# The head loads of a fused S5 scan and GEGLU kernel: w_gate in three column parts, one up row in one piece, token tile 3 earlier in the queue, and a new order of all engines

## The chip, the cores and the metric

The kernel runs on one core of a Trainium2 chip. The metric is the device time of one execution in microseconds (us). Three executions of the kernel before took 178.48 to 178.82 us, median 178.79.

## What is computed

`x` has 2048 tokens of 512 channels, all tensors are bfloat16. The reference, cut to what matters:

```python
xn  = (x - mean(x)) / sqrt(var(x) + 1e-5)            # per token
# A: a diagonal state space model over the tokens, 512 complex states
dt = exp(log_dt); Lam_bar = exp(dt * Lam)
B_bar = ((Lam_bar - 1.0) / Lam)[:, None] * Bmat
h = Lam_bar * h + B_bar @ xn[t]                      # for t = 0 .. 2047
s[t] = 2.0 * (Cmat @ h).real + xn[t] * Dskip
# B: a gated feed-forward block of 1376 columns
g = silu((gelu(xn @ w_gate) * (xn @ w_up)) @ w_down)
out = x + s * g
```

## The kernel before

**Tiling.** The tokens form 4 slabs of 512, each of 4 tiles of 128. The 1376 columns of w_gate and w_up are three chunks: 0 to 512 (chunk 0), 512 to 1024 (chunk 1, up to `W2`), and the last 352 (chunk 2). `W1` is 512.

**Slab 0's head.** Nothing is loaded when the kernel starts, so slab 0 is done in small steps. SyncE (SP) issues the loads of token tiles and weights in one queue (`load_x` L296, `load_w` L287, `load_slab` L291). The first token tile is centred by VectorE in two halves (L418), the other three get their sums from ScalarE (L423) and are centred by VectorE (L424). TensorE transposes each centred tile (L387 for tile 0 in two pairs of 128 columns, L400 for the others), VectorE or ScalarE copies the transposed tile to `W` (L391, L393, L402). Then `up_rows` (L462) multiplies one 128-row slice of w_up, one chunk and one tile per matmul, 32 in all, in an order that follows the arrival of the rows. `first_w` (L499) takes the remaining up products (chunk 2) and then all gate products of slab 0, four matmuls per tile and chunk, each group followed on ScalarE by a scaled copy (L471) or the gelu (L505) that empties its PSUM bank. `gated` (L518, VectorE) multiplies the two.

**The steady part.** From then on the tokens come normalised (`norm`, sums by ScalarE L848 for slabs 2 and 3, normalisation L853) and transposed by a DMA (`dma_t4`, L436, tile `xnT`). For each tile there are gate and up products (`gate_tile`, L536, emptied at L539), a DMA transpose of the gated activations (`at_t`, L551), and the product with w_down (`down_pair`, L564, silu at L567). For each slab `half` forms the 512 complex inputs of the scan in 16 products of four matmuls (L621) with the transposed B_re and B_im (loaded at L314); ScalarE empties their banks to `U` (L623), VectorE rotates (L638), scans (L657) and rotates back (L646 and L650) to the states `hst`. `y_part` multiplies the states with `C2` (L579), and VectorE multiplies with the silu and adds x (L586, L587) before the output DMA (L592). The last output tile of all comes in three pieces of 160, 160 and 192 columns. Tables of cosines and sines for the rotation are made early by `tables` (L707 on GpSimd, L708 on ScalarE, L719 on VectorE).

**What sets the order.** All of this is recorded as some 695 numbered steps in a class `Plan`, each with its engine, what it reads and writes, and its buffer group. `Plan.run` emits them in the order of the table `ORDER`; the table `SLOTS` gives each buffer group its buffer: `ps` six PSUM banks, `pp` two more, and the rest SBUF buffers. An engine executes its steps in exactly that order, so a step that waits holds up what stands behind it on the same engine. The queue order of the loads is set by `ORDER` too, not by the place of the `load_` call in the code.

Of the kernel before, what the change touches and what calls it, by code (L numbers as in the profile page):

```python
# [18 lines left out]


ORDER = (
# [24 lines left out]
)  # L46
SLOTS = {
# [4 lines left out]
    ),  # L52
    "pp": (
        0, 0, 1, 0, 1, 1, 0, 1, 0, 0, 1, 0, 0, 1, 1, 1, 1, 1, 0, 0, 0, 0, 0, 0, 1, 1, 1, 0, 1, 0, 0, 0, 1, 1, 0, 1, 1, 1, 1,
    ),
    "U": (
        0, 1, 2, 3, 0, 1, 2, 3,
    ),
    "g2": (
        0, 1, 4, 5, 3, 5, 1, 2, 0, 3, 4, 2, 0, 1, 5, 4,  # L60
    ),
    "at": (
        1, 0, 3, 2, 0, 2, 1, 1, 0, 3, 2, 3, 0, 2, 1, 1,
    ),
    "gtA": (
        0, 1, 1, 0, 1, 1, 0, 0, 1, 1, 0, 1, 0, 1, 0, 1,
    ),
    "gtB": (
        0, 1, 0, 1, 1, 0, 0, 1, 0, 1, 1, 1, 0, 0, 0, 1,
    ),  # L70
    "ubA": (
        1, 1, 0, 0, 1, 0, 1, 1, 1, 0, 1, 0,
    ),
    "ubB": (
        1, 1, 0, 0, 0, 1, 1, 1, 0, 0, 0, 1,
    ),
    "yg": (
        0, 1, 1, 0, 0, 0, 1, 0, 1, 1, 0, 0, 1, 0, 0, 1, 1, 0, 1,
    ),
    "ot": (  # L80
        1, 1, 0, 0, 0, 0, 0, 0, 1, 0, 0, 0, 0, 1, 1, 1, 0,
    ),
    "sk": (
        2, 3, 1, 0, 6, 5, 7, 4, 2, 1, 0, 3, 5, 6, 4, 7,
    ),
    "atT": (
        1, 0, 2, 2, 0, 1, 3, 3, 3, 0, 2, 2, 0, 3, 1, 1,
    ),
}

# [58 lines left out]
def kernel(  # L149
# [21 lines left out]
    F = 1376  # L171
    KT = D // P
# [23 lines left out]
    def sb(name, shape, dt=BF16):  # L196
        return consts.tile(shape, dt, name=name)
# [3 lines left out]
    wg = sb("wg", [P, KT, F])  # L201
    wu = sb("wu", [P, KT, F])
# [10 lines left out]
    W2 = CH[1][1]  # L213
# [51 lines left out]
    def dma(eng, issue, land, emit, reads=(), writes=(), **kw):  # L265
        return pl.add(eng, issue, emit, reads, writes, lag=land, **kw)
# [11 lines left out]
    def dma_sp(end, landed, emit, writes, **kw):  # L278

        n = dma(SP, end - sp_at[0], landed - end, emit, writes=writes, after=list(sp_last), not_before=sp_at[0], svc=(1, 0.0, 0.0), **kw)  # L280
        sp_at[0] = end
        sp_last[:] = [n]

    def load_w(nm, k0, k1, c0, c1, end, landed):

        w, r = w_of[nm]
        dma_sp(end, landed, lambda: nc.sync.dma_start(out=w[:, k0:k1, c0:c1], in_=r[:, k0:k1, c0:c1]),  # L287
               [(nm, k, c) for k in range(k0, k1) for c in range(3) if c0 <= CH[c][0] < c1])
# [6 lines left out]
    def load_x(m, end, landed):  # L295
        dma_sp(end, landed, lambda: nc.sync.dma_start(out=x_tok[:, m, :], in_=x_r[:, m, :]), [("x", 0, m)])  # L296

    W1 = CH[0][1]
# [5 lines left out]
    load_w("wu", 1, 2, 0, W1, 3.47, 5.5)  # L304
    load_w("wu", 1, 2, W1, W2, 3.94, 6.05)
    load_x(3, 4.41, 6.6)
    load_w("wu", 2, 3, 0, W1, 4.88, 7.15)
    load_w("wu", 2, 3, W1, W2, 5.35, 7.7)
    load_w("wu", 3, 4, 0, W2, 5.82, 8.8)
    load_w("wu", 0, KT, W2, F, 6.29, 10.0)  # L310
    load_w("wg", 0, KT, W1, F, 6.76, 12.4)
    load_w("wg", 0, KT, 0, W1, 7.23, 14.0)
    for ri, src in enumerate((A_B_re, A_B_im)):
        dma(SP, 2.0, 3.0, lambda ri=ri, src=src: nc.sync.dma_start_transpose(out=BT[:, ri, :, :], in_=src), writes=[("BT", ri)],  # L314
            after=list(sp_last), svc=TURN)
# [614 lines left out]
```

## Time and profile before

| | |
|---|---|
| median of three runs | 178.79 us (178.48 to 178.82) |
| the profiled execution | 179.01 us |
| its span, first to last instruction | 177.2 us |
| TensorE busy | 172.8 us (97%) |
| VectorE busy | 155.0 us (87%) |
| ScalarE busy | 125.7 us (71%) |
| GpSimd busy | 10.7 us (6%) |

The profile is of one execution and starts its clock at the first instruction; 1.81 us of the execution's own time lie around the span. Its views: the chain of work that ended last, followed back from the last instruction; the timeline, in which each row is a run of like instructions on one engine (start, length, line, number, and in brackets the idle time ahead with what ended it); the busy time of each engine in chosen windows; and the DMA issues with the median time to landing. "SPq" is the issue of a DMA by SyncE, "PEld" a weight load of TensorE, which runs beside its matmuls. Two timeline rows of pipelined instructions can overlap, so the distance of two starts says more than a length.

### The profile page before, as it was taken

The numbers are of one execution on the slowest core, as the hardware profiler recorded it, in microseconds if no ns is written. First come the engines' busy times: TensorE is split into PE (matmuls) and PEld (weight loads), VectorE is DVE, ScalarE is ACT, GpSimd is POOL, SyncE is SP. The second block draws the span as 40 slices with busy tenths as digits, with TensorE's granted clock in tenths as the row PEclk, the third lists the DMA queues.
The fourth block names the chain that finished last, engine by engine and source line by source line (L and its number), as shares of the span: only waits on it lengthen the run. The fifth ranks groups of instructions, "written<-read, shape, count | busy, mean of one in ns | idle before, by whom it ended". The sixth has DMA issues, their size and how long they took to land.

```text
span 177.2 us, 2445 instructions
## 1 busy us (share of the span) xinstructions
PE 172.8 (97%) x857; PEld 82.6 (47%) x857; DVE 155.0 (87%) x255; ACT 125.7 (71%) x242; POOL 10.7 (6%) x25
## 2 busy tenths in 40 slices
PE   7999999999999999999999999999999999999993
PEld 2444544454544444445455444444454454444452
DVE  3651989999999999999999999999995999999543
ACT  6698999999898999574877715796439394936200
POOL 2650210000010000020000000000000000000000
PEclk9999999999999999999999999999999999999999
DMA  5899998999807542005442000290004206640531
GB/s 151 259 297 254 189 225 174 215 257 282 118 0 136 108 85 37 0 0 111 103 87 45 31 0 0 58 209 11 30 0 119 52 0 85 141 83 0 111 104 44
DMA packets 48467, 18.66 MB, mean 105 GB/s; under 512 B 40424, under 2 KB 48328, under 8 KB 48456
## 3 DMA queue, kind: packets, MB, share of 16 engines
q1 hardware_dynamic: 48432, 18.52, 49.0%
q8 instruction: 6, 0.10, 0.2%
q14 instruction: 5, 0.04, 0.1%
q10 hardware_dynamic: 24, 0.00, 0.0%
HBM read 6.46 MB, written 2.10 MB: 48 GB/s over the span
## 4 chain that ended last, share of the span: by engine, by line
PE 90%; DMA 4%; SPq 3%; issue 0%; DVE 0%
PE bank L536 32%; PE bank L564 21%; PE bank L579 16%; PE bank L621 16%; PE bank L499 6%; DMA wg<-in_B_w_gate_dram 4%; SPq L287 2%; SPq L296 1%; DVE yg L586 0%; DVE ot L587 0%
## 5 line engine op out<-in xcount | busy, mean ns | idle before, releaser
L536 PEld LDWEIGHTS <-xnT 128*128 128x128 bf16 x288 | 28.2, 98 | 29.2 <-issue 0.2
L564 PE MATMUL bank<-wd,atT 128*128 128x512 bf16 (+1 forms) x176 | 39.8, 379 | 0.0
L536 PE MATMUL bank<-wg,xnT 128*128 128x512 bf16 (+1 forms) x144 | 32.3, 357 | 0.0
L536 PE MATMUL bank<-wu,xnT 128*128 128x512 bf16 (+1 forms) x144 | 31.8, 357 | 0.0
L621 PE MATMUL bank<-xnT,BT 128*128 128x512 bf16 x128 | 30.7, 379 | 0.0
L657 DVE TENSOR_TENSOR_SCAN Fs<-rho,ini,W 128x512 bf16<-128x512 f32 x24 | 30.0, 1273 | 0.1
L579 PE MATMUL bank<-C,hst 128*128 128x512 bf16 (+2 forms) x144 | 29.8, 355 | 0.0
L564 PEld LDWEIGHTS <-atT 128*128 128x128 bf16 (+1 forms) x176 | 17.2, 98 | 20.4
L623 ACT ACTIVATE U<-bank 128x512 bf16<-128x512 f32 x32 | 18.8, 613 | 7.9 <-PE bank L621 7.9
L567 ACT ACTIVATE g<-bank 128x512 f32<-128x512 f32 x16 | 9.3, 599 | 16.2 <-PE bank L564 16.2
L539 ACT ACTIVATE gtA<-bank 128x512 bf16<-128x512 f32 x24 | 14.1, 604 | 9.3 <-PE bank L536 4.9
L579 PEld LDWEIGHTS <-hst 128*128 128x128 bf16 x144 | 13.5, 98 | 13.9
L621 PEld LDWEIGHTS <-BT 128*128 128x128 bf16 x128 | 12.5, 98 | 14.3
L638 DVE TENSOR_TENSOR Q<-U,tab 128x4096 bf16<-128x4096 bf16 x8 | 18.3, 2286 | 0.1
L638 DVE TENSOR_TENSOR Q<-Fs,tab 128x4096 bf16<-128x4096 bf16 x8 | 18.3, 2286 | 0.1
L539 ACT ACTIVATE ubA<-bank 128x512 bf16<-128x512 f32 x24 | 14.5, 604 | 3.8 <-PE bank L536 3.8
L586 DVE TENSOR_TENSOR yg<-bank,g 128x512 bf16<-128x512 f32 (+2 forms) x18 | 11.2, 624 | 4.9 <-PE bank L579 3.4
L575 ACT ACTIVATE bank<-sk 128x512 f32<-128x512 bf16 (+2 forms) x18 | 10.0, 562 | 1.1 <-DVE yg L586 1.1
L848 ACT ACTIVATE junk<-x_tok 128x512 bf16<-128x512 bf16 x16 | 10.3, 650 | 0.0
L499 PE MATMUL bank<-wg,W 128*128 128x512 bf16 (+1 forms) x48 | 9.8, 357 | 0.4 <-DMA wg<-in_B_w_gate_dram 0.4
L853 ACT ACTIVATE xna<-x_tok,nb,rs 128x512 bf16<-128x512 bf16 x12 | 9.4, 816 | 0.2 <-DVE nb L866 0.2
L657 DVE TENSOR_TENSOR_SCAN Fs<-rho,W 128x512 bf16<-128x512 f32 x8 | 9.2, 1205 | 0.0
(120 smaller groups left out, 178.4 us busy)
## 6 DMA issues: line engine op xcount, KB each, us to landing
out_dram<-ot SPq DMA_DIRECT2D x15, 128.0 KB, 1.7
x_tok<-in_A_x_dram SPq DMA_DIRECT2D x3, 512.0 KB, 9.6
wd<-in_B_w_down_dram SPq DMA_DIRECT2D x1, 1280.0 KB
wg<-in_B_w_gate_dram SPq DMA_DIRECT2D x1, 864.0 KB
wu<-in_B_w_up_dram SPq DMA_DIRECT2D x6, 128.0 KB, 2.5
x_tok<-in_A_x_dram SPq DMA_DIRECT2D x4, 128.0 KB, 2.2
wg<-in_B_w_gate_dram SPq DMA_DIRECT2D x1, 512.0 KB, 8.8
wu<-in_B_w_up_dram SPq DMA_DIRECT2D x1, 352.0 KB, 5.0
```

The lines of the kernel that those rows point to most:

```text
L499: T.matmul(ps[:, 0 : b - a], lhsT=xcT[:, k, m * P : (m + 1) * P], rhs=wt[:, k, a:b], start=(k == 0), stop=(k == KT - 1))
L536: T.matmul(ps[:, 0 : b - a], lhsT=xnT[:, s % 2, m, k, :], rhs=wt[:, k, a:b], start=(k == 0), stop=(k == KT - 1))
L539: acts(b - a, lambda: act(out=dst, in_=ps[:, 0 : b - a], func=AF.Copy if up else AF.Gelu_apprx_tanh), [key], [ok], table=None if up else " ...
L564: T.matmul(ps[:], lhsT=atT[:fs, k, iT * P : (iT + 1) * P], rhs=wd[:fs, k, :], start=(k == 0), stop=(k == NFT - 1))
L575: acts(w, lambda: act(out=ps, in_=skt[:, c0:c1], func=AF.Copy), [kk], [key])
L579: T.matmul(ps, lhsT=hst[s % 2][:, j // NPT, j % NPT, m * P : (m + 1) * P], rhs=C2[:, j // NPT, j % NPT, c0:c1], start=False, stop=(j == 2 ...
L586: dve(w, lambda: V.tensor_tensor(out=yg[iy][:, 0:w], in0=ps, in1=g2[ig][:, c0:c1], op=ALU.mult), [key, ("g2", gg)], [("yg", gy)])
L621: T.matmul(ps[:], lhsT=BT[:, ri, k, pt * P : (pt + 1) * P], rhs=xnT[:, s % 2, :, k, :], start=(k == 0), stop=(k == KT - 1))
L623: acts(512, lambda q=q, ri=ri, ps=ps: act(out=U[ui][:, ri, q, :], in_=ps[:], func=AF.Copy), [key], [("U", ug, q, ri)])
L638: dve(4096, lambda: V.tensor_tensor(out=Qf, in0=src.unsqueeze(1).to_broadcast(WQ), in1=table, op=ALU.mult), reads, ["Q"], rate=2.0)
L657: pl.add(DVE, 1.12 if s == 0 else 1.185, lambda ri=ri, q=q, pt=pt, first=first: V.tensor_tensor_scan(out=Fs[:, ri, q, :], data0=rho[:, pt ...
L848: acts(512, lambda i=i, fn=fn, sc=sc, m=m: act(out=junk()[:], in_=x_tok[:, s * M + m, :], func=fn, scale=sc, accum_out=sx[:, s, i, m : m + ...
```

## The change

Two calls of `load_w` become one, one becomes two, and `ORDER` and `SLOTS` are replaced as a whole. The diff without the two tables:

```diff
     load_x(3, 4.41, 6.6)
-    load_w("wu", 2, 3, 0, W1, 4.88, 7.15)
-    load_w("wu", 2, 3, W1, W2, 5.35, 7.7)
+    load_w("wu", 2, 3, 0, W2, 5.35, 7.7)
     load_w("wu", 3, 4, 0, W2, 5.82, 8.8)
     load_w("wu", 0, KT, W2, F, 6.29, 10.0)
-    load_w("wg", 0, KT, W1, F, 6.76, 12.4)
+    load_w("wg", 0, KT, W1, W2, 6.76, 12.4)
     load_w("wg", 0, KT, 0, W1, 7.23, 14.0)
+    load_w("wg", 0, KT, W2, F, 7.7, 15.0)
```

The third up row (index 2, 256 KB for chunks 0 and 1) is loaded in one transfer instead of two. w_gate is loaded as its middle 512 columns (512 KB), its first 512 (512 KB), its last 352 (352 KB); before, the middle and the last came together (864 KB) and then the first. The number of loads ahead of slab 1 stays 14. All the engines' orders are new. Three places follow.

SyncE's queue from the start to slab 0's transposed B (`x_tok` tokens, `wu` and `wg` the weights; `x3` means three like instructions), as a piece of the difference:

```order
 L296 DMA x_tok_63<-in_A_x_dram 128x512 x3
-L287 DMA wu_66<-in_B_w_up_dram 128x512 x6
+L287 DMA wu_66<-in_B_w_up_dram 128x512 x4
 L296 DMA x_tok_63<-in_A_x_dram 128x512
-L287 DMA wu_66<-in_B_w_up_dram 128x1024
+L287 DMA wu_66<-in_B_w_up_dram 128x1024 x2
 L287 DMA wu_66<-in_B_w_up_dram 128x4x352
-L287 DMA wg_65<-in_B_w_gate_dram 128x4x864
-L287 DMA wg_65<-in_B_w_gate_dram 128x4x512
+L287 DMA wg_65<-in_B_w_gate_dram 128x4x512 x2
+L287 DMA wg_65<-in_B_w_gate_dram 128x4x352
 L291 DMA x_tok_63<-in_A_x_dram 128x4x512
```

The load of token tile 3 (the single L296) stands two issues earlier, ahead of all of up row 2. Further down, the load of slab 2 (a second L291, from 23.10 us in the profile before) goes ahead of a small load of w_down (L773) that it stood behind.

VectorE at its start as it was before the change (`xna` the centred tokens, `bank` a PSUM bank, `W` the transposed tokens; the memsets write constants, L686 casts parameters):

```order
L414 TENSOR_SCALAR yg0_111,ma_138<-x_tok_63 128x320
L325 MEMSET mhalf_128 128x4
L418 TENSOR_SCALAR xna_96<-x_tok_63,ma_138,mb_139 128x256 x2
L686 CAST pf_149<-bank1_119 128x12
L424 TENSOR_SCALAR xna_96<-x_tok_63,ma_138 128x512
L391 COPY W_93<-bank3_121 128x2x128
L326 MEMSET e_t_130 128x4
```

And the same place of VectorE's list after the change:

```order
L414 TENSOR_SCALAR yg0_111,ma_138<-x_tok_63 128x320
L418 TENSOR_SCALAR xna_96<-x_tok_63,ma_138,mb_139 128x256 x2
L391 COPY W_93<-bank1_119 128x2x128
L326 MEMSET e_t_130 128x4
L424 TENSOR_SCALAR xna_96<-x_tok_63,ma_138 128x512
L324 MEMSET halfpi_127 128x1
```

The copy of tile 0's transposed half (L391) moved ahead of the centring of tile 1 (L424), the cast of the parameters behind it. On TensorE the four transposes of tile 1 (L400) and the second pair of tile 0's (L387) stand ahead of the first up product in both orders, with those of tile 1 now first.

ScalarE where slab 0's scan inputs begin, before the change (`gtA`, `gtB` the gelu's outputs, `U` the scan inputs, `sx` the sums of slab 2):

```order
L853 ACTIVATE xna_96<-x_tok_63,nb_137,rs_136 128x512
L505 ACTIVATE gtA1_81<-bank2_120,rs_136 128x512
L623 ACTIVATE U0_88<-bank4_122 128x512
L623 ACTIVATE U0_88<-bank3_121 128x512
L505 ACTIVATE gtA1_81<-bank0_118,rs_136 128x512
L623 ACTIVATE U1_89<-bank1_119 128x512
L505 ACTIVATE gtB0_82<-bank7_125,rs_136 128x352
L471 ACTIVATE at3_79<-bank6_124,rs_136 128x352
L623 ACTIVATE U0_88<-bank3_121 128x512
L623 ACTIVATE U0_88<-bank2_120 128x512
L848 ACTIVATE junk0_116,sx_169<-x_tok_63 128x512
```

The same place of ScalarE's list after the change:

```order
L853 ACTIVATE xna_96<-x_tok_63,nb_137,rs_136 128x512 x4
L505 ACTIVATE gtA0_80<-bank1_119,rs_136 128x512
L623 ACTIVATE U0_88<-bank5_123 128x512
L848 ACTIVATE junk0_116,sx_169<-x_tok_63 128x512
L505 ACTIVATE gtB1_83<-bank7_125,rs_136 128x352
L623 ACTIVATE U1_89<-bank2_120 128x512
L623 ACTIVATE U1_89<-bank4_122 128x512
L623 ACTIVATE U0_88<-bank1_119 128x512
```

The first sum over slab 2 (L848) stood behind the fifth copy to `U`; now it stands behind the first. In the whole program ScalarE has 13 table loads instead of 11, and VectorE 237 listed rows instead of 240.

More of the change, by code (lines that the diff above doesn't have):

```diff
@@ L48 @@
     "ps": (
[3 rows of a table removed]
[3 rows of a table added]
     ),
     "pp": (
-        0, 0, 1, 0, 1, 1, 0, 1, 0, 0, 1, 0, 0, 1, 1, 1, 1, 1, 0, 0, 0, 0, 0, 0, 1, 1, 1, 0, 1, 0, 0, 0, 1, 1, 0, 1, 1, 1, 1,
+        0, 0, 1, 0, 1, 0, 1, 1, 0, 0, 1, 1, 0, 0, 1, 0, 1, 1, 1, 0, 1, 0, 0, 0, 1, 0, 0, 0, 1, 1, 1, 0, 0, 1, 0, 1, 1, 1, 0,
     ),
     "U": (
-        0, 1, 2, 3, 0, 1, 2, 3,
+        1, 0, 2, 3, 0, 1, 2, 3,
     ),
     "g2": (
-        0, 1, 4, 5, 3, 5, 1, 2, 0, 3, 4, 2, 0, 1, 5, 4,
+        5, 4, 0, 1, 2, 4, 1, 3, 1, 5, 5, 0, 4, 3, 2, 1,
     ),
     "at": (
-        1, 0, 3, 2, 0, 2, 1, 1, 0, 3, 2, 3, 0, 2, 1, 1,
+        3, 1, 2, 0, 1, 0, 1, 2, 2, 3, 1, 0, 2, 0, 3, 1,
     ),
     "gtA": (
-        0, 1, 1, 0, 1, 1, 0, 0, 1, 1, 0, 1, 0, 1, 0, 1,
+        1, 0, 0, 1, 0, 1, 0, 1, 1, 0, 1, 0, 0, 1, 1, 0,
     ),
     "gtB": (
-        0, 1, 0, 1, 1, 0, 0, 1, 0, 1, 1, 1, 0, 0, 0, 1,
+        1, 1, 0, 1, 0, 1, 0, 0, 0, 0, 0, 1, 1, 1, 1, 0,
     ),
     "ubA": (
-        1, 1, 0, 0, 1, 0, 1, 1, 1, 0, 1, 0,
+        0, 0, 1, 1, 1, 0, 1, 0, 1, 1, 1, 0,
     ),
     "ubB": (
-        1, 1, 0, 0, 0, 1, 1, 1, 0, 0, 0, 1,
+        1, 1, 0, 0, 0, 0, 0, 1, 1, 0, 0, 1,
     ),
     "yg": (
-        0, 1, 1, 0, 0, 0, 1, 0, 1, 1, 0, 0, 1, 0, 0, 1, 1, 0, 1,
+        0, 0, 0, 1, 1, 0, 0, 1, 0, 1, 1, 1, 0, 1, 0, 0, 0, 1, 0,
     ),
     "ot": (
-        1, 1, 0, 0, 0, 0, 0, 0, 1, 0, 0, 0, 0, 1, 1, 1, 0,
+        0, 0, 1, 1, 0, 1, 1, 1, 0, 0, 0, 1, 1, 1, 0, 0, 1,
     ),
     "sk": (
-        2, 3, 1, 0, 6, 5, 7, 4, 2, 1, 0, 3, 5, 6, 4, 7,
+        2, 3, 1, 0, 7, 6, 5, 4, 3, 2, 1, 0, 6, 2, 5, 7,
     ),
     "atT": (
-        1, 0, 2, 2, 0, 1, 3, 3, 3, 0, 2, 2, 0, 3, 1, 1,
+        3, 0, 1, 3, 2, 1, 2, 1, 3, 0, 1, 2, 2, 3, 0, 0,
     ),
```

54 rows, old and new, of tables (ORDER, SLOTS) are left out of this document.

## The prediction, made before the changed kernel had run

> **What bounds the kernel now.** I read the page's span, then the chain of work that ended last, then the span cut into five stretches. The columns of the third fence are window, length, then busy time of TensorE (PE), its weight loads, VectorE (DVE), ScalarE (ACT) and GpSimd (POOL), the clock, DMA share and GB/s.
>
> ```profile
> span 177.2 us, 2445 instructions
> ```
> ```profile
> 6.40 7.92 DMA wg<-in_B_w_gate_dram
> 14.36 10.05 PE bank L499 x52
> ```
> ```profile
> 0.00:14.36 14.36, 12.94 (x65) 5.76 (x66) 6.77 (x29) 10.82 (x26) 6.82 (x21) 1.00 0.81 247
> 14.36:66.00 51.64, 51.64 (x254) 24.86 (x254) 47.77 (x93) 49.31 (x97) 2.92 (x3) 1.00 0.87 166
> 66.00:135.00 69.00, 69.00 (x338) 32.94 (x337) 66.71 (x86) 45.63 (x90) 1.01 (x1) 1.00 0.23 48
> 135.00:174.20 39.20, 39.18 (x203) 19.00 (x200) 33.17 (x46) 19.93 (x33) 0.00 (x0) 1.00 0.36 79
> 174.20:177.20 3.00, 0.00 (x0) 0.00 (x0) 0.62 (x2) 0.00 (x0) 0.00 (x0) 1.00 0.15 44
> ```
> From 14.36, when the first part of w_gate has landed, to 174.20 TensorE is never idle (51.64 + 69.00 + 39.18 of 159.84 us, granted clock 1.00), and 3.00 us of tail follow. So the span is (start of the first gate product) + 159.8 + 3.0. The changed kernel issues the same matmuls, as many behind that point, and the same three last pieces of output. Time can come only from the head, and be lost in a head wait or in a new TensorE stall in the body.
>
> **The head of before.** Rows of the timeline: start, length, engine, line; in brackets the idle time ahead and what ended it.
>
> ```profile
> 3.42 0.60 DVE L418 TENSOR_SCALAR xna<-x_tok,ma,mb 128x256 bf16<-128x256 bf16 x2
> 4.51 0.29 DVE L391 COPY W<-bank 128x256 bf16<-128x256 bf16 x1
> 4.73 0.35 DVE L424 TENSOR_SCALAR xna<-x_tok,ma 128x512 bf16<-128x512 bf16 x1
> 4.86 0.65 PE L462 MATMUL bank<-wu,W 128*128 128x512 bf16 x2
> 5.57 3.62 PE L462 MATMUL bank<-wu,W 128*128 128x512 bf16 x16
> 8.05 0.63 ACT L423 ACTIVATE junk<-x_tok 128x512 bf16<-128x512 bf16 x1 [1.72 <-DMA x_tok<-in_A_x_dram]
> 9.21 0.40 PE L400 MATMUL bank<-ident,xna 128*128 128x128 bf16 x4
> 9.56 3.18 PE L462 MATMUL bank<-wu,W 128*128 128x512 bf16 x14
> 12.58 1.36 PE L499 MATMUL bank<-wu,W 128*128 128x352 bf16 x8
> 14.36 6.53 PE L499 MATMUL bank<-wg,W 128*128 128x512 bf16 x32 [0.43 <-DMA wg<-in_B_w_gate_dram]
> ```
> ```profile
> 31.92 0.86 PE bank L536 x4
> 30.46 0.60 PE bank L499 x4
> ```
> A 512-column matmul advances TensorE by 0.86/4 = 0.216 us, a 352-column one by 0.60/4 = 0.150; a transpose of 128 columns by about 0.055 (0.216 x 128/512). From the first up product (4.86) to the first gate product (14.36) are 9.50 us; the work in them is 32 x 0.216 + 8 x 0.150 + 8 x 0.055 = 8.55. So **0.95 us are idle**: 14.36 - (12.58 + 8 x 0.150) = 0.58 at the end, for w_gate, and 0.37 ahead of that, most of it around the transposes of token tile 3, for which ScalarE waits 1.72 us. These are what the change can win.
>
> **The change part by part, head.** The queue of loads, of before (the last two rows are the page's: KB of each, then the median time from issue to landing):
>
> ```profile
> 2.11 2.82 SPq L287 DMA_DIRECT2D wu<-in_B_w_up_dram  x6
> 4.97 0.43 SPq L296 DMA_DIRECT2D x_tok<-in_A_x_dram  x1
> 6.40 1.05 SPq L287 DMA_DIRECT2D wg<-in_B_w_gate_dram  x2
> 7.50 1.10 SPq L291 DMA_DIRECT2D x_tok<-in_A_x_dram  x1
> wg<-in_B_w_gate_dram SPq DMA_DIRECT2D x1, 512.0 KB, 8.8
> x_tok<-in_A_x_dram SPq DMA_DIRECT2D x4, 128.0 KB, 2.2
> ```
> - *Start of the up products, +0.29.* In the new order L391's copy stands ahead of token tile 1's centring (L424), and ahead of its first up product TensorE takes that tile's four transposes, as in before, and now the second pair of tile 0's behind them. The copy starts behind L418 (3.42 + 0.60) and the transposes that it reads, at about 4.09, takes 0.29, then a memset (0.04 more) and the centring of 0.35: 4.77. With 0.05 of latency and 6 x 0.055 of transposes the first up product stands at 5.15 instead of 4.86. Bounds 0 and 0.4 (the copy as late as in before).
> - *Token tile 3, +0.10.* Its load is issued two issues of 2.82/6 = 0.47 earlier, at 4.03 instead of 4.97. In before its reader started at 8.05, 3.08 after the issue; the four token tiles' median is 2.2. So it lands at 6.2 to 7.1. Its transposes follow 1.16 behind (8.05 to 9.21): ready at 7.4 to 8.3. TensorE reaches them after four transposes and 12 matmuls behind 5.15, at 5.15 + 0.22 + 12 x 0.216 = 7.96. Stall between 0 and 0.3; I take 0.10, since with fewer bytes in front the short end is the nearer. Up row tile 2, in one piece behind it, lands where tile 3 did, about 8.0, and is wanted at 8.2.
> - *w_gate's middle part, 0.* Another 0.22 + 20 x 0.216 + 8 x 0.150 = 5.74 us bring TensorE to its first gate product at 13.80. In before 864 KB landed at 14.33, and the 512 KB behind them at 6.40 + 0.53 + 8.8 = 15.7. So 512 KB took 1.37, and a part that is 352 KB shorter is there 0.94 earlier: 13.39, before it is wanted. Any earlier costs nothing more, no earlier than in before (14.33) stalls 0.53: bounds 0 and 0.53.
> - *w_gate's first part, +0.10.* Four matmuls later, at 14.66, TensorE wants the first part; by the same line it lands at 13.39 + 1.37 = 14.76. Bounds 14.33 and 15.7, a stall of 0 to 1.04. The last part closes the same bytes by 15.7 and is wanted after 16.
>
> A page of the Trainium skill speaks against splitting: "DMA: Bandwidth & Descriptors", section "Anatomy of one DMA", gives each transfer about 2.0 us fixed plus its bytes at 436 GB/s, and its section "Bandwidth" advises 1 MiB and more per DMA. Taken as one transfer behind another, the first part would by its figures come an estimated 3.2 us after the middle one, at 16.6, and the sum would be +1.4 instead of -0.46. The rows above contradict it: 512 KB landed 1.37 us behind the transfer in front, so a fixed part, if any, overlaps.
>
> **Body.** TensorE's first gate product moves by -0.95 + 0.29 + 0.10 = -0.56, and 0.10 is lost behind it. Everything else stays only if no bank, copy or load is late. ScalarE is nearest:
>
> ```profile
> 21.39 0.73 ACT L505 ACTIVATE gtA<-bank,rs 128x512 bf16<-128x512 f32 x1
> 21.96 0.61 ACT L471 ACTIVATE at<-bank,rs 128x352 bf16<-128x352 f32 x1
> 22.39 0.75 ACT L505 ACTIVATE gtA<-bank,rs 128x512 bf16<-128x512 f32 x1
> 23.08 2.22 ACT L853 ACTIVATE xna<-x_tok,nb,rs 128x512 bf16<-128x512 bf16 x3
> 143.65 1.28 ACT L567 ACT_TABLE_LOAD   x1
> 144.94 0.60 ACT L567 ACTIVATE g<-bank 128x512 f32<-128x512 f32 x1
> ```
> One after another, a 512-column instruction on a bank takes ScalarE 0.57 (21.39 to 21.96), one of 352 columns 0.43, a normalisation 2.22/3 = 0.74. The last row product of tile 3 has two 352-column groups and two row products behind it and ends at 13.80 - 1.20 - 0.43 = 12.17; ScalarE sees it some 0.2 later, at 12.37. From there ScalarE has four copies of 512 columns, one of 352, two small ones (0.2 each), the gelu table and three gelus ahead of the first bank that TensorE wants back: 12.37 + 4 x 0.57 + 0.44 + 0.4 + 1.28 + 0.1 + 2 x 0.57 + 0.44 = 18.45, with 0.1 to TensorE 18.55. TensorE comes for it after four gate products of 512 columns more than the first and one of 352, and the 0.10: 13.80 + 5 x 0.86 + 0.60 + 0.10 = 18.82. Slack 0.27. Adding the ScalarE and VectorE rows in the new order against TensorE's in the same way, I find no negative slack: bank slacks of 0.06 (the first state products) to 0.3, as small as in before; the states of slabs 0 to 3 ready 2 to 3.5 us before wanted; the transposed activations 1.5 us. The two more table loads of 1.28 us fall into ScalarE's idle time (69.00 - 45.63 + 39.20 - 19.93 = 42.6 us from 66 on): 0. The queue issues 14 loads ahead of slab 1 as before, so nothing behind them is issued later: 0. VectorE's three fewer rows and POOL's exchanged casts lie under these slacks: 0. If that cover is gone, each 0.1 us of lateness is 0.1 us of time.
>
> The Trainium skill, "ScalarE: Activation LUTs", section "What ACT_TABLE_LOAD costs", adds some 1.38 us of drain to each load. Here the activation starts at 144.94, 0.01 behind the load's end (143.65 + 1.28): no drain is seen, and by the page the two would still lie in the idle time, so that the sum is the same.
>
> **Sum.** -0.95 + 0.29 + 0.10 + 0 + 0.10 = **-0.46 us**: span 177.2 to 176.7, the profiled execution (179.01, 1.81 more than its span) to 178.55. It was 0.22 above the median of the runs, 178.79, which I take down by the same 0.46: **178.3**. With the head's stalls at nothing: -0.95 + 0.29 = -0.66 (178.1), without the late start 177.9. The other end is a first part that lands at 15.7, whatever stalled before it: TensorE stood at 14.36 + 0.86 = 15.22 at that point in before, so +0.48 (179.3).
>
> **Rivals.**
>
> *Gain eaten by what isn't moved.* Slab 0's state products (L621) wait for the transposed loads of B_im and B_re, and the row products for xn transposed:
>
> ```profile
> 20.50 1.92 SPq L314 DMA_TRANSPOSE BT<-in_A_B_re_dram  x1
> 24.25 6.21 PE L621 MATMUL bank<-xnT,BT 128*128 128x512 bf16 x28
> DMA to landing us min/median/max: 4.6/4.9/5.3
> ```
> The last row is that of the transposed token tile. If B_re takes 4.6 to 5.3 it is there at 25.1 to 25.8; before, the first product with it stood two products behind 24.28, at 26.0, in the change it would at 25.55. So up to 0.25 of the 0.46 goes here, and all of it if the load really ended at 26.0. For it: this queue does not start earlier, since slab 1 in front lands no earlier with the same bytes. Against: nothing waited in before. Time 178.6 to 178.8. The other form, that w_gate comes no sooner for being cut, gives 178.8 too.
>
> *Slower: slab 2's rows under the U copies.* The load of x slab 2 and its first reader, of before:
>
> ```profile
> 23.10 0.42 SPq L291 DMA_DIRECT2D x_tok<-in_A_x_dram  x1
> 27.05 1.07 ACT L623 ACTIVATE U<-bank 128x512 bf16<-128x512 f32 x2
> 31.46 0.63 ACT L848 ACTIVATE junk<-x_tok 128x512 bf16<-128x512 bf16 x1
> x_tok<-in_A_x_dram SPq DMA_DIRECT2D x3, 512.0 KB, 9.6
> 27.00:28.00 1.00, 1.00 (x7) 0.47 (x5) 0.97 (x2) 1.00 (x3) 0.00 (x0) 1.00 0.23 57
> ```
> In the new order ScalarE reads slab 2 (L848) behind its second instruction after the four normalisations: 18.45 + 3 x 0.44 + 6 x 0.57 + 4 x 0.74 + 2 x 0.57 = 27.3, 4.2 earlier than in before, and the U copies that free TensorE's banks stand behind it. The load goes out 0.64 earlier (22.46), ahead of a small load of w_down instead of behind it. From a landing at about 27.4 on (27.3 and the 0.06 of slack) each microsecond is one of TensorE's. With the median 9.6 it lands at 32.1: 4.7 us, 183.0. Against: it was no later than 31.46 in before, and the DMA share falls to 0.23 at 27, so what was issued before is mostly through. A landing at 28.4 gives +0.5, 179.3.
>
> *Slower: w_gate's first part no sooner than in before*, at 15.7: +0.48 as worked out above, 179.3; it decides from a landing at 15.22 on. Were each transfer's latency paid apart, 2.2 us (the small loads' median) and the 512 KB's 1.37 behind 13.39 would be 16.9: 1.7 behind 15.22, 180.5. This is the mechanism of the Trainium skill's fixed cost above.
>
> **Chances.** Forecast (177.9 to 178.6) 0.45; eaten, or w_gate no sooner (178.6 to 179.0) 0.23; slab 2 late 0.14 (179.2 to 183); w_gate's first part late 0.10 (0.02 of it for latencies paid apart); some other bank or load of the new order late 0.08. 0.2% is 0.36 us, about what a measurement of this kernel can tell from no change: faster ends at 178.43, slower starts at 179.15. The forecast's upper edge and the eaten case fall into "same": faster 0.42, same 0.28, slower 0.30. The range leaves out most of the slab-2 case and a little below: 177.9 to 179.8; the likeliest alone 177.9 to 178.6.
>
> **What would show it.** Right: the first up product near 5.15, token tile 3's sums at 6.2 to 7.1 on ScalarE, the first gate product near 13.8 with at most 0.2 idle ahead of it and of the next bank, TensorE 160 us without a gap, tail 3.0. Wrong: an idle bracket "DMA x_tok" at L848 near 27 with TensorE waiting at L621; "DMA wg" at 14.7; "DMA BT" or "DMA xnT" at L621 or L536; TensorE idle behind ScalarE's L505 near 18.8; or any stall between 66 and 174, which I exclude only by sums of rows.

## The result and the profile after

The changed kernel is **slower**: 180.88 us median of 6 runs (179.21 to 181.21) against 178.73 for the kernel before (178.32 to 179.01), ratio 1.010 with a 95% interval of 1.0075 to 1.0125. The prediction said 178.3, and its range ended at 179.8.

The profiled execution of the changed kernel took 181.21 us, with this span:

```profile
span 179.4 us, 2427 instructions
```

The head of TensorE in the changed kernel, from the timeline (start, length, engine, line; in brackets the idle time ahead and what ended it):

```profile
0.76 3.15 PE L375 MATMUL bank<-const-bfloat16-1.0 128*128 128x512 bf16 x7 [0.76 <-PEq L914]
3.99 0.39 PE L387 MATMUL bank<-ident,xna 128*128 128x128 bf16 x2
4.31 0.18 PE L683 MATMUL bank<-ident,pv 4*128 4x4 bf16 x1
4.36 0.16 PE L684 MATMUL bank<-ident,pv 8*128 8x8 bf16 x1
5.04 0.61 PE L400 MATMUL bank<-ident,xna 128*128 128x128 bf16 x4 [0.52 <-DVE halfpi L324]
5.44 0.42 PE L387 MATMUL bank<-ident,xna 128*128 128x128 bf16 x2
5.66 0.63 PE L462 MATMUL bank<-wu,W 128*128 128x512 bf16 x1
6.08 0.63 PE L400 MATMUL bank<-ident,xna 128*128 128x128 bf16 x4
6.51 4.28 PE L462 MATMUL bank<-wu,W 128*128 128x512 bf16 x11
10.63 0.39 PE L400 MATMUL bank<-ident,xna 128*128 128x128 bf16 x4
10.85 4.05 PE L462 MATMUL bank<-wu,W 128*128 128x512 bf16 x17
...
15.77 0.76 PE L499 MATMUL bank<-wu,W 128*128 128x352 bf16 x4
16.36 1.89 PE L499 MATMUL bank<-wg,W 128*128 128x512 bf16 x8
```

Read the distances of the starts. From 6.51 to 10.63 TensorE takes 4.12 us for 11 matmuls, 0.37 each, and nothing is waited for. From 10.85 on 18 of the same matmuls (the row lists 17, one record is missing) take 3.89, 0.216 each. Four transposes take 0.43 at 6.08 and 0.22 at 10.63. So **TensorE runs at two paces**: 0.427 us per 512-column matmul (5.66 to 6.08 holds one of 0.42) and 0.216. If 11 matmuls take 4.12, then (4.12 - 11 x 0.216) / 0.211 = 8.3 of them were slow, and the pace changed at about 6.51 + 8.3 x 0.427 = 10.0.

The 0.52 us ahead of 5.04 are a wait for tile 1's centring on VectorE (L424; the bracket names the memset that ends with it). In the kernel before that centring starts at 4.07, ahead of the copy L391 at 4.51; in the changed kernel it stands behind the copy and ends at 4.99. First the row of before, then two of after:

```profile
4.07 0.35 DVE L424 TENSOR_SCALAR xna<-x_tok,ma 128x512 bf16<-128x512 bf16 x1
```
```profile
4.42 0.29 DVE L391 COPY W<-bank 128x256 bf16<-128x256 bf16 x1 [0.23 <-PE bank L387]
4.64 0.35 DVE L424 TENSOR_SCALAR xna<-x_tok,ma 128x512 bf16<-128x512 bf16 x1
```

The slow pace was there to be read in the kernel before too, in the products on constants at its start (L375), whose starts lie 0.43 us apart:

```profile
L375 PE MATMUL bank<-const-bfloat16-1.0 x7: 464/631/631, 0.8 to 3.3; 128*128 128x512 bf16 x7
L462 PE MATMUL bank<-wu,W x32: 376/379/389, 4.9 to 12.4; 128*128 128x512 bf16 x32
```

The rows are the group of these products and that of the up products in the kernel before: least, median and longest duration of one in ns, then first and last start. The last of the seven products lasted 464 ns instead of 631, so the pace changed inside it, at about 3.4 us, well ahead of the up products, of which none was slow. In the changed kernel the group of up products has a longest of 635:

```profile
L462 PE MATMUL bank<-wu,W x31: 379/379/635, 5.7 to 15.6; 128*128 128x512 bf16 x31
```

The clock column does not show it. In two windows of the changed kernel it stands at 1.00 (third number from the end) while four matmul records lie in or reach into one microsecond and seven into another:

```profile
9.00:10.00 1.00, 1.00 (x4) 0.38 (x3) 0.00 (x0) 0.00 (x0) 0.83 (x3) 1.00 0.80 251
11.00:12.00 1.00, 1.00 (x7) 0.46 (x5) 0.91 (x4) 0.00 (x0) 0.00 (x0) 1.00 1.09 364
```

The packed trace's own record of the granted clock, from which the column is made, does show it: its first entry, full clock, stands at 10.04 us in the changed kernel and at 3.44 in the kernel before, and the column counts the time ahead of the first entry as 1.00. The only other value in these records is 0.5, behind TensorE's last product (from 177.52 us on in the kernel before).

**Where the 2.2 us of span went.** The first gate product starts at 16.36 instead of 14.36: 2.00. From there to the last run of y products (172.25 in the kernel before, 174.46 now) are 158.10 us instead of 157.89: 0.21. The tail is the same. The 0.21 is found in one place, on TensorE and ScalarE of the changed kernel near 127:

```profile
123.27 1.28 ACT L567 ACT_TABLE_LOAD   x1
124.56 0.60 ACT L567 ACTIVATE g<-bank 128x512 f32<-128x512 f32 x1
125.05 0.59 ACT L623 ACTIVATE U<-bank 128x512 bf16<-128x512 f32 x1
125.66 1.28 ACT L539 ACT_TABLE_LOAD   x1
126.96 0.46 ACT L539 ACTIVATE gtB<-bank 128x352 bf16<-128x352 f32 x1
```
```profile
126.38 1.03 PE L621 MATMUL bank<-xnT,BT 128*128 128x512 bf16 x4
127.47 0.76 PE L536 MATMUL bank<-wu,xnT 128*128 128x352 bf16 x4
```

The four matmuls at 126.38 advance TensorE by 0.86, to 127.24; the next start at 127.47. Between, ScalarE loads the silu table for a single silu and then the gelu table again, and the gelu that empties the bank comes late (126.96 to 127.42).

The loads did not lose anything. All waits of TensorE that the profile names in the changed kernel are these two, none for a DMA:

```profile
PE bank L375 <- PEq L914: 0.8, 1, 0.8
PE bank L400 <- DVE halfpi L324: 0.5, 1, 0.5
```

Of the three parts of w_gate, whose issues start at 5.92, half a microsecond apart, the landings of the first and the last are on record, 5.9 and 7.3 us behind their issues (the median is the mean of the two):

```profile
DMA to landing us min/median/max: 5.9/6.6/7.3
```

### The profile page after: what moved, and what is told of

Read it like the earlier page. It is cut to its first block, busy times and chain, and to the rows that moved or that the text cites. A ratio compares the mean times of both kernels' runs of the same rounds, so it can differ in the third digit from the quotient of the medians.

```text
span 179.4 us, 2427 instructions
## 1 busy us (share of the span) xinstructions
PE 174.1 (97%) x841; PEld 83.7 (47%) x857; DVE 154.8 (86%) x255; ACT 128.1 (71%) x244; POOL 10.3 (6%) x25
## 4 chain that ended last, share of the span: by engine, by line
PE 89%; ACT 6%; DVE 2%; DMA 1%; issue 1%; DVEq 0%
PE bank L536 29%; PE bank L564 21%; PE bank L579 14%; PE bank L621 13%; PE bank L499 6%; PE bank L462 5%; DMA x_tok<-in_A_x_dram 1%; ACT U L623 1%; ACT gtA L539 1%; ACT L539 1%; ACT L567 1%; PE bank L400 1%; ACT bank L575 1%; ACT gtB L539 0%; DVE at L518 0%
## 5 line engine op out<-in xcount | busy, mean ns | idle before, releaser
L848 ACT ACTIVATE junk<-x_tok 128x512 bf16<-128x512 bf16 x16 | 11.0, 708 | 0.0
L539 ACT ACTIVATE ubB<-bank 128x352 bf16<-128x352 f32 x12 | 5.9, 498 | 5.8 <-PE bank L536 5.8
```

Of the source, the lines that this page charges most:

```text
L539: acts(b - a, lambda: act(out=dst, in_=ps[:, 0 : b - a], func=AF.Copy if up else AF.Gelu_apprx_tanh), [key], [ok], table=None if up else " ...
```

## The experiments

The theory after the result, called the pace theory: TensorE works at half pace until it has worked for some microseconds without a hole. The new order puts a hole of 0.52 us (4.52 to 5.04) into that stretch when the pace hasn't changed by then, so the change comes at about 10. (The expectations put the change in the kernel before at about 4.8, where its up products start; in its profiled execution it stands at 3.44.) Two rivals: that the up rows arrive more slowly because token tile 3 goes ahead of them (queue theory), and that the loss is in banks and copies of the new order (order theory). All ratios are to the kernel before, run on the same chip; its median was 178.88 to 178.99. A ratio is the recorded one and need not be that of the two medians.

### e1_fill: the changed kernel with its hole filled

```diff
         def f():
+            T.matmul(ps[:], lhsT=warm[:, 0:P], rhs=warm, start=True, stop=True)
             T.transpose(pt_ps[:, 0:4], pv0[:, :], ident[0:4, 0:4])
```

> The changed kernel with one idle-filling matmul of 512 columns on constants ahead of the parameter transposes, in the bank that these overwrite. Pace theory (TensorE runs its matmuls at half pace until it has worked for some microseconds without a hole; the hole of 0.52 us at 4.5 in the changed kernel puts the change of pace off from about 4.8 to about 10): the up products run at 0.216 us each from about 5 on, the first gate product stands at 13.8 to 14.4 instead of 16.36, the time is 178.3 to 179.0 and the scatter of the runs shrinks. Queue theory (the up rows arrive later or more slowly because token tile 3 goes ahead of them, and the matmuls stretch over their arrival): nothing gets faster, 180.5 to 181.3. Order theory (banks and copies of the new order): as the queue theory.

Measured: 179.31 us median (178.69 to 180.55, 10 runs), ratio 1.0027 (1.0002 to 1.0052). Its profiled execution took 178.83, span 177.0:

```profile
4.90 0.40 PE L400 MATMUL bank<-ident,xna 128*128 128x128 bf16 x4 [0.31 <-DVE halfpi L324]
5.13 0.28 PE L387 MATMUL bank<-ident,xna 128*128 128x128 bf16 x2
5.24 0.38 PE L462 MATMUL bank<-wu,W 128*128 128x512 bf16 x1
5.46 0.39 PE L400 MATMUL bank<-ident,xna 128*128 128x128 bf16 x4
5.68 2.54 PE L462 MATMUL bank<-wu,W 128*128 128x512 bf16 x11
8.12 0.40 PE L400 MATMUL bank<-ident,xna 128*128 128x128 bf16 x4
```

One added matmul of useless work, and the 11 up products take 2.44 us (5.68 to 8.12) instead of 4.12. The first gate product stands at 13.94 instead of 16.36. In this execution full clock had come at 3.96, ahead of the 0.31 us that are left of the hole, so it alone could be a lucky one. The ten runs say more: no span is above 178.0, while 11 of the 18 runs of the changed kernel (those of e12_again included) have spans of 178.7 to 179.6. The queue theory is out: the loads are those of the change. The median is above what was expected, and the scatter stayed wide; part of it lies outside the span (in 3 of the 10 runs 2.1 to 3.0 us lie around it instead of 1.7 to 2.0).

### e4_gap: the kernel before with the hole

```diff
-    39, 45, 35, 19, 65,
+    39, 35, 45, 19, 65,
```

(Step 35 is the copy L391, step 45 the centring of tile 1.)

> The kernel before with one pair of VectorE steps exchanged: the copy of tile 0's transposed half (L391) ahead of the centring of tile 1 (L424), as the change has it; loads and everything else as before. TensorE then waits some 0.6 us ahead of tile 1's transposes. Pace theory: the up products run at half pace until 8 to 10 us and the time is 180 to 181.3 in most runs. Queue and order theories: the start of the up products moves by 0.3 to 0.6 and the idle time behind takes most of it up: 178.8 to 179.3.

Measured: 180.36 (178.96 to 180.96, 8 runs), ratio 1.0056 (1.0021 to 1.0091). The runs fall into two groups: three at 178.96 to 179.17 and five at 180.31 to 180.96. The profile is of the upper group:

```profile
5.41 0.61 PE L400 MATMUL bank<-ident,xna 128*128 128x128 bf16 x4 [0.65 <-DVE e_t L326]
5.81 1.06 PE L462 MATMUL bank<-wu,W 128*128 128x512 bf16 x2
6.67 0.63 PE L400 MATMUL bank<-ident,xna 128*128 128x128 bf16 x4
7.09 4.85 PE L462 MATMUL bank<-wu,W 128*128 128x512 bf16 x16
11.78 0.39 PE L400 MATMUL bank<-ident,xna 128*128 128x128 bf16 x4
```

Exchanging two VectorE steps, with nothing else changed, brings the slow pace into the kernel before: 16 matmuls in 4.69 us, so 5.9 of them slow and the pace changed at 9.6 (9.57 by the clock record).

### e3_order and e2_loads: the two halves of the change

e3_order has the order and slots of the change on the old loads:

```diff
-    6, 5, 7, 8, 9, 10, 11, 12, 13, 151,
+    6, 5, 8, 9, 7, 10, 11, 12, 13, 151,
```

> The order and the slots of the change alone, with the loads of before in their old cut and queue order. Pace theory: the hole is there, so the up products run at about 0.43 us until about 10 and the time is 180.4 to 181.3, with some runs near 179. Queue theory: the rows come as in before, so 178.5 to 179. Order theory: 180.4 to 181.3, but with up products at 0.216 us each and the loss as waits on banks.

Measured: 180.80 (180.31 to 182.64, 4 runs), ratio 1.012 (1.0052 to 1.0188). The up products run slowly again, up to 634 ns, and the first gate product stands at 16.38. The order alone makes the whole loss.

e2_loads has the loads of the change under the order of before (step 7 is token tile 3; 11, 12, 13 are w_gate's parts):

```diff
-    6, 5, 8, 9, 7, 10, 11, 12, 13, 151,
+    6, 5, 7, 8, 9, 10, 11, 13, 12, 151,
```

> The loads of the change alone: the order and the slots of before, with token tile 3 two issues earlier, up row 2 in one piece and w_gate in three parts (middle, last, first, since the order of before uses the last part second). Pace theory: TensorE has no hole at 4.5, the pace changes near 4.8 as in before, and the head gains up to 0.95 us of idle time: 178.0 to 178.6. Queue theory: the up products stretch, 180 to 181. Order theory: as the pace theory.

Measured: 179.33 (178.78 to 179.84, 10 runs), ratio 1.0011 (0.9988 to 1.0034): no difference. The pace is full from 4.86 on, and TensorE no longer waits for w_gate, but for w_up, twice:

```profile
5.55 0.38 PE L462 MATMUL bank<-wu,W 128*128 128x512 bf16 x1 [0.31 <-DMA wu<-in_B_w_up_dram]
...
8.45 1.89 PE L462 MATMUL bank<-wu,W 128*128 128x512 bf16 x8 [0.57 <-DMA wu<-in_B_w_up_dram]
```

What w_gate gives (0.58) the up rows take back; the first gate product stands at 14.61 in this execution, against 14.36.

### e5_swap: the changed kernel with the VectorE pair put back

```diff
-    33, 34, 35, 19, 45, 17, 47,
+    33, 34, 45, 35, 19, 17, 47,
```

> The changed kernel with one pair of VectorE steps put back: the centring of tile 1 (L424) ahead of the copy of tile 0's transposed half (L391), as before; loads and all else as changed. Pace theory: the hole ahead of tile 1's transposes shrinks from 0.52 to 0.2 or 0.3 us, the up products run at 0.216 us from about 5 on in most runs, the first gate product stands near 13.7, time 178.3 to 179.0 with perhaps a few runs near 180. If the hole is not the cause but something else in the new order of the head: 180 to 181.

Measured: 179.30 (179.02 to 179.65, 10 runs), ratio 1.0026 (1.0015 to 1.0038). No run came above 179.65, where five of e4_gap's eight stood above 180.3: with this one pair put back no run is in the upper group. In the profiled one the pace changes at 5.08, just ahead of the first up product.

```profile
4.51 0.61 PE L400 MATMUL bank<-ident,xna 128*128 128x128 bf16 x4
4.91 0.36 PE L387 MATMUL bank<-ident,xna 128*128 128x128 bf16 x2
5.11 0.38 PE L462 MATMUL bank<-wu,W 128*128 128x512 bf16 x1
...
8.72 0.40 PE L400 MATMUL bank<-ident,xna 128*128 128x128 bf16 x4 [0.48 <-DVE at L328]
```

Once TensorE is fast it waits 0.48 us for tile 3, which the slow pace had hidden.

### e6_swapfill: pair put back and hole filled

The diffs of e1_fill and e5_swap together.

> The kernel of the expectation above with the idle-filling matmul on constants ahead of the parameter transposes as well, so that TensorE has no hole of more than about 0.1 us from 0.8 on. Pace theory: full pace in every run, first gate product near 13.7, median 178.3 to 178.6 and a scatter below 0.8 us: faster than both kernels. If the scatter of the other runs has another source than the pace: as wide as theirs, 178.5 to 180.5.

Measured: 179.46 (178.37 to 180.54, 10 runs), ratio 1.0029 (1.0007 to 1.0051). Not as expected: no faster than e5_swap, with a wider scatter, though the spans lie between 176.6 and 177.8; in 2 runs about 1 us more lies around the span. Full pace is not all that the changed kernel lacks.

### e8_nodummy: the kernel before without its warm-up

```diff
-    dummies(7)
+    dummies(1)
```

> The kernel before with 1 instead of 7 of the products on constants that TensorE runs at its start (they enter no output), so TensorE's steady work starts near 3.7 us instead of 0.8. Pace theory: the up products run at 0.43 us until at least 7.1 (3.4 us of steady work, the time the runs so far put between the first work and the change of pace) and up to 10.5, time 179.7 to 181.3. If the pace has nothing to do with earlier work, nothing changes: 178.7 to 179.1.

Measured: 179.93 (179.56 to 180.54, 4 runs), ratio 1.0061 (1.0037 to 1.0084). Steady work starts at 4.19 instead of 0.76:

```profile
6.44 4.68 PE L462 MATMUL bank<-wu,W 128*128 128x512 bf16 x16
10.96 0.39 PE L400 MATMUL bank<-ident,xna 128*128 128x128 bf16 x4
```

16 matmuls take 4.52, so 5.1 are slow and the pace changes at 8.6 (8.57 by the clock record), 4.4 us behind the start of steady work. By then TensorE had worked about 5 us in all; in the changed kernel it had worked 8.8 when its pace changed. So what counts is not the sum of the work; a stretch of it without a large hole fits both.

### e9_copy: without the two added table loads

On top of the edit of e5_swap, the kernel leaves out the silu of slab 2's tile 1, which enters the output:

```diff
-            acts(512, lambda i=i, ps=ps: act(out=g2[i][:], in_=ps[:], func=AF.Silu), [key], [("g2", g)], table="silu", rank=3.0)
+            fn = AF.Copy if (s, m) == (2, 1) else AF.Silu
+            acts(512, lambda i=i, ps=ps, fn=fn: act(out=g2[i][:], in_=ps[:], func=fn), [key], [("g2", g)], table="silu", rank=3.0)
```

> The changed kernel with the VectorE pair put back, and one silu of sixteen (slab 2, tile 1) left out: its instruction copies instead, so that ScalarE needs neither of the two table loads around it (11 loads instead of 13; everything else, the copy's 0.6 us too, stays). Table theory (the 0.22 us that TensorE stands idle near 125 in every run of the new order is these two loads): the wait is gone, the stretch from the first gate product to TensorE's end is 159.8 instead of 160.05, and the time is 0.2 to 0.3 us below that of the kernel with the pair put back. If the loads are hidden, as the prediction had it, and the wait has another cause: it stays, and the time does not move.

Measured: 179.07 (178.78 to 179.70, 12 runs) against 179.30 for e5_swap, both beside a kernel before at 178.88; ratio 1.0022 (1.0009 to 1.0034), which overlaps with that of e5_swap, so the timing alone does not decide. The profile does. In e5_swap, then in e9_copy (whose lines stand one further down):

```profile
124.49 1.03 PE L621 MATMUL bank<-xnT,BT 128*128 128x512 bf16 x4
125.58 0.61 PE L536 MATMUL bank<-wu,xnT 128*128 128x352 bf16 x3
```
```profile
124.16 1.03 PE L622 MATMUL bank<-xnT,BT 128*128 128x512 bf16 x4
125.03 0.76 PE L536 MATMUL bank<-wu,xnT 128*128 128x352 bf16 x4
```

The distance is 1.09 with the loads and 0.87 without, and from the first gate product to the last run of y products are 157.89 us (14.13 to 172.02), as in the kernel before, instead of 158.11.

### e7_split, e10_splitfill, e11_fill0: is there a gain in the loads?

e7_split has the order of before, with up row 2 in one piece ahead of tile 3 and w_gate in three parts:

```diff
-    6, 5, 8, 9, 7, 10, 11, 12, 13, 151,
+    6, 5, 8, 7, 9, 10, 11, 13, 12, 151,
```

> The order and slots of before, w_gate in three parts (middle, last, first) and up row 2 in one piece, but that row ahead of token tile 3 in the queue, as in before. If the move of tile 3 made the up rows late in the run with all the loads of the change (0.31 and 0.57 us of waiting for w_up): no wait for w_up, no wait for w_gate either, time 178.2 to 178.6. If the single piece of 256 KB makes row 2 late wherever it stands: a wait for w_up of 0.3 to 0.6 us stays and the time is that of before, 178.8 to 179.1.

Measured: 178.96 (178.38 to 179.21, 10 runs), ratio 1.0000 (0.9986 to 1.0015). In its profile there is no wait for w_up and none for w_gate, but the pace changes only at 6.5 in that execution, which gives the rows more time, and the first gate product stands at 14.37. So the next kernel fills the hole of 0.2 us that the order of before has at 3.9 (one 256-column matmul on constants behind the parameter transposes), and another does so in the kernel before:

> Order of before, w_gate in three parts (middle, last, first), up row 2 in one piece ahead of token tile 3, and a 256-column matmul on constants behind the parameter transposes, which fills the hole of 0.2 us at 3.9 that the kernel before has too. Pace theory: the pace changes by 4.8 in every run instead of at times at 6.5 to 7, there is no wait for w_gate, first gate product at 13.8 to 14.0, median 178.3 to 178.6, faster than the kernel before. If the hole of 0.2 us does no harm: as without the filling, 178.8 to 179.0.

> The kernel before with the same filling of its hole at 3.9 and nothing else. Pace theory: the first gate product still waits for w_gate at 14.3, so the median stays at 178.7 to 178.9; only runs above 179.2 become fewer. If full pace alone were the gain: 178.3.

Measured: 178.75 (178.52 to 179.22, 12 runs), ratio 1.0000 (0.9989 to 1.0010), and 178.70 (178.35 to 179.19, 12 runs), ratio 0.9995 (0.9983 to 1.0008). The profile of e10_splitfill has the first gate product at 13.95, 0.41 ahead of before, with a span of 176.8, but over the runs nothing of it can be measured. Its 16 up products behind 5.71 take 3.80 us (up to the next transposes at 9.51) instead of 16 x 0.216 = 3.46: two of them start just behind the landings of up rows, at 7.14 and 7.79, so at full pace up rows still come late by 0.34 in all, also with row 2 ahead of tile 3. No version that beats the kernel before was found.

### e12_again: the changed kernel once more

> The changed kernel itself once more, for the scatter of its runs. Pace theory with windows: a window of 3.4 us that starts behind 0.76 and ends ahead of the hole at 4.5 fits in few of the runs, so about one run in ten to one in five stands near 179.2, the others between 180 and 181.3. If the slow pace came in every run: all between 180.5 and 181.3.

Measured: 180.57 (179.21 to 181.42, 12 runs), ratio 1.0078 (1.0050 to 1.0107). The runs stand in two groups: five at 179.21 to 179.41, seven at 180.44 to 181.42, with none between. (Of the six runs of the result one is in the lower group, at 179.21, four are in the upper, and one stands between, at 179.93.) The slow pace isn't in every run, as expected, but the share of the lower group (5 of 12) is more than the window model gave.

## Why the prediction was wrong

**The step that failed is "Start of the up products, +0.29".** It saw that the copy L391 ahead of the centring makes TensorE start later, and it charged only the delay, with 0.216 us for each matmul whatever came before. The hole that this opens is itself 0.52 us, and in the profiled executions the change of pace comes at 10.04 instead of 3.44: the term came to +0.80 and brought 2.16 behind it. e5_swap takes the long slow stretch out of the changed kernel with this pair alone, and e4_gap puts it into the kernel before. No rival had this mechanism, although two paces stood in the profile of before (0.43 for the products on constants, 0.216 for the up products).

The sum, term by term, against the span of the profiled executions:

| term | predicted | measured | how |
|---|---|---|---|
| idle time of the old head | -0.95 | -0.95 | no wait for tile 3 or w_gate is left |
| start of the up products | +0.29 | +0.80 | 4.86 to 5.66; 0.16 of it is the first token tile, which landed later in that execution (L414 at 2.97 instead of 2.81), and 0.29 the six transposes at slow pace (5.04 to 5.66, instead of 6 x 0.055) |
| slow pace behind that | not seen | +2.16 | 0.21 for the first product, 0.21 for four transposes, 1.74 for the eleven |
| tile 3 | +0.10 | 0 | hidden under the slow pace; 0.48 in e5_swap, 0.16 in e9_copy |
| w_gate's middle and first part | +0.10 | 0 | last part in at about 14.3, no wait |
| body | 0 | +0.21 | the table loads |
| sum | -0.46 | +2.2 | |

**The loads were judged rightly in kind and too gloomily in size.** In e1_fill, at full pace, the first gate product stands at 13.94, where 13.80 was forecast. The parts of w_gate were forecast for 13.4, 14.8 and 15.7; the first landed at 11.8, and the last was issued at 7.0 and took 7.3. The rule of the Trainium skill that was weighed ("DMA: Bandwidth & Descriptors", "Anatomy of one DMA — SWDGE (gpsimd) path") is a fit to transfers that GpSimd issues, about 2.0 us fixed and the bytes at 436 GB/s. SyncE issues these loads; read as a rule for them too, one transfer behind another, it would put the last part an estimated 6.0 us behind the first. The trace has 2.5 us between the two landings (11.81 and 14.27), so nothing of a fixed part is seen. But e2_loads adds what the prediction had at nothing: TensorE waits 0.31 and 0.57 us for up rows. The 0.57 is for up row 2, which lands behind tile 3 there. The 0.31 is for a row issued ahead of tile 3, at 2.59, whose landing differs between executions (5.51 there, 5.09 in the kernel before, 5.43 in e11_fill0 with the loads of before), so it is not shown to come from the change of the queue. The gain of the loads alone is given back where it is made.

**The body was wrong by one term.** "Two more table loads fall into ScalarE's idle time: 0" counted ScalarE's idle time over 108 us. The loads stand in a place where ScalarE has none: 0.22 us, shown by e9_copy. The rivals did not happen: slab 2's sums (L848, at 29.71) and the state products show no wait in the changed kernel.

**What the pace depends on.** The Trainium skill, "TensorE: Matmul & The Clock Gate", "Part 1: The HAM clock gate", describes it: the clock is halved until a window of about 3.4 us has been busy, and the windows run freely, not from the kernel's start. The runs agree in the two paces (0.427 and 0.216 us). The clock records put full clock at 3.39 to 6.48 us where no large hole stands ahead of it (least in e6_swapfill, most in e7_split), at 9.23 to 10.16 in the four profiled executions with the slow stretch behind a hole of 0.52 or 0.65 (the changed kernel, e12_again, e3_order, e4_gap), and at 8.57 in e8_nodummy; e9_copy has no entry. So it comes 2.6 to 5.7 us behind the start of such a stretch (0.76 to 3.39, 0.76 to 6.48, 4.19 to 8.57, 5.04 to 10.04), at a time that differs between executions, and the hole can do harm only where the change has not come before it; this fits the groups of runs of one kernel. With the page's windows I had put the share of the lower group at one in ten to one in five; e12_again had 5 of 12. I had counted only windows without any idle time, and the 2.6 us show that a window need not be busy from end to end: by the page's 3.4 us, the one that ended at 3.39 in e6_swapfill held an estimated 0.78 us ahead of the first product. How much idle time a window tolerates stays open: holes of 0.52 and 0.65 us did harm in most runs, of 0.2 to 0.3 in few or none (one of the 23 runs of the kernel before beside e1_fill to e4_gap stood at 180.47, with a span of 178.7).

**What stays open.** With full pace and without the table loads (e9_copy) the changed kernel is still 1.0022 (1.0009 to 1.0034) of the kernel before, and its own lower group (179.21 to 179.41) stands above the median of 178.88 too. Its profiled execution is one of its fastest (span 177.0) and shows no cause; other runs may wait longer in the head, for tile 3 as in e5_swap's profile, but that is argued and was not tried.

## What to carry to other kernels

Before costing a shift of work in the first microseconds, compare the pace of like matmuls along the head: if the first ones take twice as long as the later ones, a hole in TensorE's early work can cost not only itself but half the time of every matmul up to the next change of pace, here 2.2 us for a hole of 0.5. And time that an engine has idle over a long stretch hides nothing at one place: ask for the slack of the next instruction behind the added work, as the 0.22 us behind two table loads show.

## What the runs showed of the hardware that was not expected

TensorE's half pace leaves no mark in the clock column, which reads 1.00 throughout; the durations show it (635 ns against 379 for one matmul record, 0.427 against 0.216 us from start to start), and so does the place of the clock record's first entry. And the outcome of one and the same program is mostly in two groups, 179.2 to 179.4 and 180.4 to 181.4 us (17 of 18 runs), by which a comparison of few runs can be misled. A matmul of no use, 0.4 us long and placed ahead of the hole, took the median from 180.88 to 179.31.
